# Gradient of w_mod in an adaLN block: its sixth row moved behind the last fold, four rows of the last stage on VectorE

## The chip, the cores and the metric

The kernel runs on one core of a Trainium2 chip. A core has five engines with instruction queues of their own: TensorE (PE, matrix products, with the weight load PEld), VectorE (DVE), ScalarE (ACT), GpSimd (POOL) and SyncE (SP, which here only issues DMA transfers; POOL and ACT issue some too). An engine works through its queue in order; an instruction that waits holds up all behind it. Queues wait for each other through semaphores. The metric is the device time of one execution in microseconds, the median of several runs.

## The reference, cut to what matters

The kernel computes the forward pass and all gradients of one block with x of 2048 x 1024 tokens in bf16:

```python
mod = (_silu(c) @ w_mod).reshape(c.shape[0], 6, 1, -1)
sa, ca, ga, sb, cb, gb = (mod[:, k].copy() for k in range(6))
h = _layernorm(x) * (1 + ca) + sa
x = x + ga * irfft2(rfft2(h) * (w_r + 1j * w_i))
h = _layernorm(x) * (1 + cb) + sb
x = x + gb * (gelu(_layernorm(h) @ w1 + b1) @ w2 + b2)
...
_out, _vjp = jax.vjp(_f, A_x, A_w_r, A_w_i, B_w1, B_b1, B_w2, B_b2, c, w_mod)
```

(`...` marks what is left out.) The change concerns the last two gradients. With u = silu(c) and g_r the gradient of the r-th of the six vectors sa, ca, ga, sb, cb, gb (1024 numbers each), the gradient of `w_mod` is, for each row r of the six, the outer product of u and g_r (1024 x 1024), and the gradient of c needs, for each row r, the product of w_mod's r-th block with g_r.

## The kernel before

The forward part is followed by the backward part, in which PE has one matrix product after another. Three stages matter here.

*Fold stage* (about 940 to 1000 us): the last of four quarters of the token gradients is brought back through the two layer norms (`ln_bwd`, by DVE reduces and ACT instructions with result in `got`), folded by DVE for the Fourier products (`fold_quarter`, whose last instruction is `fold_end`), and turned (`turn_tokens`). `make_fm` then scales the small matrices `fm` on DVE. Meanwhile PE computes products of the gradient of `w2` (`gw2acc`), one unit at a time, wherever the code says `fill(n)`: `pieces()` is a generator of such units, and every `fill` takes some. Each product of 16 matmuls goes into one of four PSUM tiles of tag `f` and is evicted from there by ACT (or, early on, DVE) into `gwo` or `gwoE`.

*Spectral core* (to about 1180): Fourier products, with `U` (CE, SE from ACT's copies of `pu`; CO, SO from DVE sums of `smbf`), the pairs with `ws` and `cs01b`, and the gradient of the filter.

*Last stage* (1185 to the end): `consume_bwd(i, ...)` finishes the four token quarters i = 0 to 3. In each, DVE unfolds, multiplies by the normalised x (`tmp = o4 * n1`, the column-sum product), goes back through the first layer norm (`scaled_rows`, `ln_bwd`) and adds `d_gx1`, which SP loads into the place of `n1` (tile `xt`, line 1483). PE fills with the 56 products of the gradient of `w1` (`gw1acc`, line 1553), each 16 matmuls into a PSUM tile of tag `f`; ACT evicts each into one of eight slots `gwo` (line 1557), and POOL stores it (line 1559). The operands `gzh` and `gzu` come by transposing transfers on SP (line 1502).

Row 3 of the gradient of `w_mod` is done in the spectral core (`row3`). The five others stand in the last stage, in `gmod_steps`: for each row r SP loads g_r, spread over the partitions, into `gr` (line 1172), and then there are eight steps of 128 lines of `w_mod`. A step loads 128 x 1024 numbers of `w_mod` into one of four slots `wrw` (line 1176); makes the outer product, u as a scale per partition times `gr`, into a slot of `otl` (rows 2, 4, 5 on ACT, line 1179, behind the last eviction, three slots; rows 1, 0 on DVE, line 1181, two slots); stores it through POOL (line 1182); and reduces `wrw` times `gr` on DVE into one column of `gu` (line 1183). Two chains, rows 5, 4, 2 and rows 1, 0, are taken in turn, a step of each per `fill(1)` from the ninth on.

Between the two stands row 0's own gradient: PE sums columns into `accSA`, ACT scales that into `sr` (line 1607). `sr` lies in the place (`px0`) that `xt` of quarter 3 had.

The order on each engine follows from the order in the code and a scheduler; `tc.issue_after(x)` keeps an instruction behind x on its own engine's order, `tc.high_priority()` moves evictions ahead. Tiles of the pool `reg` have a tag each, one place per tag: a new tile of a tag waits until the earlier one is done with.

Of the kernel before, what the change touches and what calls it, by code (L numbers as in the profile page):

```python
# [35 lines left out]
def kernel(  # L36
# [157 lines left out]
    def tt(out, a, b, op):  # L194
        return nc.vector.tensor_tensor(out=out, in0=a, in1=b, op=op)  # L195
# [975 lines left out]
    def gmod_steps(r, wrs, gws, gr):  # L1171
        nc.sync.dma_start(out=gr, in_=d_gmod[r * D:(r + 1) * D].partition_broadcast(P))
        for jc in range(NDC):
            wr, gw = wrs[:, wring[0] % 4, :], gws[jc % len(gws)]
            wring[0] += 1
            nc.sync.dma_start(out=wr, in_=w_mod[jc * P:(jc + 1) * P, r * D:(r + 1) * D])
            if r > 1:
                with tc.issue_after(w1g["ev"].ins):
                    nc.scalar.activation(out=gw, in_=gr, func=ACT.Identity, scale=u_rt[:, jc:jc + 1])  # L1179
            else:  # L1180
                nc.vector.tensor_scalar(out=gw, in0=gr, scalar1=u_rt[:, jc:jc + 1], scalar2=None, op0=ALU.mult)
            nc.gpsimd.dma_start(out=out_9[jc * P:(jc + 1) * P, r * D:(r + 1) * D], in_=gw)  # L1182
            nc.vector.tensor_tensor_reduce(out=wr, in0=wr, in1=gr, scale=1.0, scalar=0.0,  # L1183
                                           op0=ALU.mult, op1=ALU.add, accum_out=gu[:, r, jc:jc + 1])
            yield
# [59 lines left out]

    def ln_bwd(g, gsum, n_ap, tmp, order=ExitStack):
        sc = small.tile([P, 1], FP32, tag="lbsc", bufs=4)
        nc.vector.tensor_tensor_reduce(out=tmp, in0=g, in1=n_ap, scale=-1.0 / D, scalar=0.0,  # L1248
                                       op0=ALU.mult, op1=ALU.add, accum_out=sc[:])
        with order():  # L1250
            nc.scalar.activation(out=tmp, in_=n_ap, func=ACT.Identity, scale=sc[:], bias=gsum)  # L1251
        tt(g, g, tmp, ALU.add)
# [163 lines left out]
    def make_fm():  # L1416
        for r in range(2):
            cos, ncos = al[:, 1, r:r + 1], al[:, 4, r:r + 1]
            for k in range(2):
# [3 lines left out]
                for t in range(2):  # L1423
                    nc.vector.tensor_scalar(out=fv[:, t, :, 1, :], in0=em2[:, 2 + r + 4 * t, 255:P - 1:-1].rearrange("p (h j) -> p h j", h=2),
                                            scalar1=cos if t == k else ncos, scalar2=None, op0=ALU.mult)

# [33 lines left out]
    css2 = reg.tile([P, 2, 2, 2 * PW], BF16, name="cs01b", tag="px0")  # L1460
    with tc.issue_after(gx_in[0].ins):
        nc.gpsimd.memset(css2[:], 0.0)
    accCA = []

    def consume_bwd(i, o4, tmp, tmp2, n1, eb):
# [10 lines left out]
        tt(tmp, o4, n1, ALU.mult)  # L1476
# [6 lines left out]
        nc.sync.dma_start(out=n1, in_=chunk_rows(d_gx1, i))  # L1483
        tt(o4, o4, n1, ALU.add)
        store_tok(out_1, o4, i)
        fill((4, 1, 2, 2)[i])
# [19 lines left out]
    def pieces():  # L1506
# [34 lines left out]
        w1g["gr"] = reg.tile([P, 2, D], BF16, name="gr", tag="sb")  # L1541
        w1g["gr2"] = reg.tile([P, 2, D], BF16, name="gr2", tag="gm")
# [29 lines left out]
    for cl in (CE, SE):  # L1572
        nc.sync.dma_start(out=smA2[:, cl // 2], in_=d_SF[:, cl])
    sums3(3, gn3s[1], pru)
    nc.sync.dma_start(out=em2, in_=d_E[:, 0])
    fill(8)
    with tc.issue_after(fold_end[0].ins):
        make_fm()
# [27 lines left out]
    for h in range(2):  # L1606
# [54 lines left out]
```

## Time and profile before

| what | value |
|---|---|
| median of 3 runs | 1410.78 us |
| lowest and highest run | 1408.07 and 1412.80 us |
| profiled execution | 1409.95 us |
| its span, first to last instruction | 1407.9 us |
| mean granted clock of TensorE | 0.992 |
| data moved by DMA | 331.12 MB, 235 GB/s over the span |

In a row of the timeline there stand: start in the span, duration, engine, line, operation, output and inputs, and how many instructions were merged; in square brackets how long the engine stood idle before, and what ended it. In a row of the windows: the window, its length, busy time of PE, PEld, DVE, ACT and POOL with their numbers of instructions, TensorE's granted clock as a share of full speed, the DMA engines' busy share, and GB/s. In a row of the waits: who waited for whom, microseconds in total, how often, the longest. In a row of the groups: line, engine, operation, shapes and count; busy time and mean ns of one; idle time before, and what ended it.

### The profile page before, as it was taken

The page shows a single profiled execution, that of the slowest core. Times are in us where ns is not written, and L with a number is a line of the kernel's source. Part 1 is how long each engine was busy: PE and PEld are TensorE (multiplying, and loading weights), DVE is VectorE, ACT ScalarE, POOL GpSimd, SP SyncE. Part 2 cuts the span into 40 slices and gives each one's busy share as a digit, 9 for nine tenths or more (in the row PEclk, how much of TensorE's full clock was granted, in tenths as well). Part 3 has the DMA queues.
Part 4 walks back from the last instruction along what each step waited for, and adds up shares of the span by engine and source line. Part 5 has one row for each costly group of instructions (what it writes and reads, how often), then busy time and mean ns, then how long its engine had stood idle before and what let it go on. Part 6 is the DMA issues. An engine that isn't in the chain of part 4 may idle for free. (4 is left out here: it accounts for less than half of the span.)

```text
span 1407.9 us, 18600 instructions
## 1 busy us (share of the span) xinstructions
PE 1360.4 (97%) x6899; PEld 655.9 (47%) x6899; DVE 1058.4 (75%) x1455; ACT 783.1 (56%) x1106; POOL 344.1 (24%) x434
## 2 busy tenths in 40 slices
PE   4898999999999999999999999999999999999888
PEld 2445565444444444444444444444645564544333
DVE  5897889977888787887620578889687679877871
ACT  4775657667867766665314593443623555443335
POOL 5410523201212122112211011111254130322333
PEclk9999999999999999999999999999999999999999
DMA  9972746799787777697999599995399697879884
GB/s 315 287 235 65 199 135 197 253 302 357 243 254 227 236 239 242 191 275 249 279 283 242 153 245 321 264 258 146 119 287 262 164 284 184 228 197 232 280 304 175
DMA packets 360688, 331.12 MB, mean 235 GB/s; under 512 B 207962, under 2 KB 303088, under 8 KB 360470
## 3 DMA queue, kind: packets, MB, share of 16 engines
q1 hardware_dynamic: 319702, 204.96, 55.7%
q0 software_dynamic: 35136, 119.73, 24.5%
q10 hardware_dynamic: 5760, 5.25, 1.2%
q8 instruction: 54, 0.88, 0.3%
q14 instruction: 36, 0.29, 0.1%
HBM read 165.73 MB, written 114.87 MB: 199 GB/s over the span
## 5 line engine op out<-in xcount | busy, mean ns | idle before, releaser
L839 PE MATMUL pp<-gBoT,wt 128*128 128x512 bf16 x896 | 198.6, 380 | 2.5 <-ACT phr L845 1.2
L1130 PE MATMUL pg<-w1T,gzr 128*128 128x512 bf16 x896 | 195.8, 379 | 0.0
L1553 PEld LDWEIGHTS <-n3n 128*128 128x128 bf16 x896 | 88.6, 99 | 120.2 <-issue 19.5
L1553 PE MATMUL gw1acc<-gzh,n3n 128*128 128x512 bf16 x640 | 140.0, 379 | 1.2 <-ACT gwo L1557 1.2
L976 PEld LDWEIGHTS <-w 128*128 128x128 bf16 x896 | 87.3, 98 | 107.7 <-issue 3.3
L839 PEld LDWEIGHTS <-wt 128*128 128x128 bf16 x896 | 87.6, 98 | 106.7 <-issue 5.2
L1130 PEld LDWEIGHTS <-gzr 128*128 128x128 bf16 x896 | 86.6, 98 | 108.4 <-issue 5.5
L976 PE MATMUL pz<-n3Tb,w 128*128 128x512 bf16 x448 | 99.2, 379 | 1.9 <-DVE w2sD L1052 1.9
L976 PE MATMUL pz<-n3Ta,w 128*128 128x512 bf16 x448 | 98.7, 379 | 0.0
L195 DVE TENSOR_TENSOR ct<-ct 128x2048 bf16<-128x2048 bf16 (+1 forms) x84 | 91.4, 1117 | 5.6 <-DMA d_n<-ct 3.1
L1030 PEld LDWEIGHTS <-hhA 128*128 128x128 bf16 x608 | 59.0, 98 | 73.1 <-issue 2.9
L1294 PE MATMUL gw2acc<-gB,hhsA 128*128 128x512 bf16 x416 | 92.4, 379 | 0.0
L979 ACT ACTIVATE gt<-pz,b_col 128x512 bf16<-128x512 f32 x112 | 72.8, 683 | 33.3 <-PE pz L976 33.0
L987 ACT ACTIVATE gt<-gt 128x2048 bf16<-128x2048 bf16 x28 | 53.5, 1911 | 64.6 <-DVE gt L195 64.6
L195 DVE TENSOR_TENSOR gt<-gt,gt 128x2048 bf16<-128x2048 bf16 x56 | 68.6, 1224 | 19.8 <-ACT gt L989 18.5
L1302 ACT CAST gwo<-gw2acc 128x512 bf16<-128x512 f32 x40 | 23.5, 588 | 87.5 <-PE gw2acc L1294 70.3
L1553 PE MATMUL gw1acc<-gzu,n3n 128*128 128x512 bf16 x256 | 60.9, 402 | 9.3 <-ACT gwo L1557 9.2
L1294 PEld LDWEIGHTS <-hhsA 128*128 128x128 bf16 x416 | 40.8, 98 | 47.1
L1183 DVE CUSTOM_DVE_ANT_0 wrw<-wrw,gr 128x1024 bf16<-128x1024 bf16 x40 | 48.0, 1219 | 18.8 <-DMA wrw<-in_w_mod_dram 18.4
L1557 ACT CAST gwo<-gw1acc 128x512 bf16<-128x512 f32 x56 | 32.0, 575 | 50.3 <-PE gw1acc L1553 42.3
L983 ACT ACTIVATE gt<-gt 128x2048 bf16<-128x2048 bf16 x28 | 53.5, 1910 | 3.2 <-DVE hhC L195 2.4
L989 ACT ACTIVATE gt<-gt 128x2048 bf16<-128x2048 bf16 x28 | 53.4, 1907 | 0.4
(367 smaller groups left out, 2515.0 us busy)
## 6 DMA issues: line engine op xcount, KB each, us to landing
gzr<-d_gz SPq DMA_DIRECT2D x28, 512.0 KB
wblk<-in_w_mod_dram SPq DMA_DIRECT2D x12, 1024.0 KB
out_dram<-otl POOLq DMA_DIRECT2D x48, 256.0 KB
d_ph<-pho POOLq DMA_DIRECT2D x21, 512.0 KB
wrw<-in_w_mod_dram SPq DMA_DIRECT2D x40, 256.0 KB
d_hh<-hhA POOLq DMA_DIRECT2D x19, 512.0 KB
w<-in_B_w_dram SPq DMA_DIRECT2D x7, 1024.0 KB
hhC<-d_ph SPq DMA_DIRECT2D x14, 512.0 KB
```

The costliest lines, as they stand in the source:

```text
L195: return nc.vector.tensor_tensor(out=out, in0=a, in1=b, op=op)
L839: last_pe[0] = nc.tensor.matmul(pp[:], lhsT=wt[:, fc % 4, cch, :], rhs=gBoT[j][:, cch, :], start=(cch == 0), stop=(cch == NDC - 1))
L976: last_pe[0] = nc.tensor.matmul(pz[:], lhsT=w1s[g][:, cch, k * P:(k + 1) * P], rhs=n3T[:, cch, :], start=(cch == 0), stop=(cch == NDC - 1))
L979: z_in = nc.scalar.activation(out=zb[:, k, :], in_=pz[:], func=ACT.Identity, bias=b1_col[:, fc:fc + 1], scale=1.0)
L983: nc.scalar.activation(out=av, in_=zb, func=ACT.Square)
L987: nc.scalar.activation(out=sg, in_=bv, func=ACT.Sigmoid, scale=2.0 * GK)
L989: nc.scalar.activation(out=bv, in_=bv, func=ACT.Sigmoid, scale=-2.0 * GK)
L1030: last_pe[0] = nc.tensor.matmul(pbs[i][:], lhsT=hh[:, k, i * P:(i + 1) * P], rhs=wp[:, k, :], start=False, stop=(g == 6 and k == 3))
L1130: last_pg[0] = nc.tensor.matmul(pgs[i][:], lhsT=gzs[b, g][:, k, i * P:(i + 1) * P], rhs=w1Ts[g][:, k, h * KH:(h + 1) * KH], start=(g == 0 ...
L1183: nc.vector.tensor_tensor_reduce(out=wr, in0=wr, in1=gr, scale=1.0, scalar=0.0, op0=ALU.mult, op1=ALU.add, accum_out=gu[:, r, jc:jc + 1])
L1294: nc.tensor.matmul(acc[:], lhsT=hh_of(fc)[:, t, :], rhs=gBs[t // 4][:, t % 4, h * KH:(h + 1) * KH], start=(t == 0), stop=(t == NT - 1))
L1553: nc.tensor.matmul(acc[:], lhsT=n3ns[t // 4][:, t % 4, cch * P:(cch + 1) * P], rhs=gz2[t // 8][:, t % 8, :], start=(t == 0), stop=(t == NT ...
```

## The change

Row 5 leaves the last stage. Its `gr5` and the first four loads of `w_mod` (`wr5a`) are issued on SP behind the loads of `smf`, the other four (`wr5b`) behind a load of the `w2` product. Its eight outer products are made on ACT behind the last `ln_bwd` instruction of the fold stage, into four slots `gw5`, and stored by POOL; its eight reduces stand on DVE behind `make_fm`. The memset of `css2` on POOL goes behind the last of those stores.

Rows 4, 2, 1, 0 become one chain, `gmod_chain`: all outer products and reduces on DVE, five slots of `otl` for all, four of `wrw`, and the load for step n + 4 issued with step n. Its first four loads stand on SP behind the `xt` load of quarter 1. The steps stand behind the column-sum product of quarter 3 on DVE: two per `fill(1)` for the first eight, one for the other sixteen.

```diff
-    def gmod_steps(r, wrs, gws, gr):
...
+    def gmod_chain(rows):
+        steps = [(r, k, jc) for k, r in enumerate(rows) for jc in range(NDC)]
+
+        def load(n):
+            r, k, jc = steps[n]
+            if jc == 0:
+                nc.sync.dma_start(out=w1g["gr"][k], in_=d_gmod[r * D:(r + 1) * D].partition_broadcast(P))
+            nc.sync.dma_start(out=w1g["wr"][:, n % 4, :], in_=w_mod[jc * P:(jc + 1) * P, r * D:(r + 1) * D])
+
+        for n in range(4):
+            load(n)
+        yield
+        for n, (r, k, jc) in enumerate(steps):
+            wr, gw, gr = w1g["wr"][:, n % 4, :], w1g["gw"][n % 5], w1g["gr"][k]
             nc.vector.tensor_tensor_reduce(out=wr, in0=wr, in1=gr, scale=1.0, scalar=0.0,
                                            op0=ALU.mult, op1=ALU.add, accum_out=gu[:, r, jc:jc + 1])
+            nc.vector.tensor_scalar(out=gw, in0=gr, scalar1=u_rt[:, jc:jc + 1], scalar2=None, op0=ALU.mult)
+            nc.gpsimd.dma_start(out=out_9[jc * P:(jc + 1) * P, r * D:(r + 1) * D], in_=gw)
+            if n + 4 < len(steps):
+                load(n + 4)
             yield
...
-    with tc.issue_after(gx_in[0].ins):
-        nc.gpsimd.memset(css2[:], 0.0)
...
+    chain = gmod_chain((4, 2, 1, 0))
...
-        tt(tmp, o4, n1, ALU.mult)
+        prod_in[0] = tt(tmp, o4, n1, ALU.mult)
...
-        nc.sync.dma_start(out=n1, in_=chunk_rows(d_gx1, i))
+        x1_in = nc.sync.dma_start(out=n1, in_=chunk_rows(d_gx1, i))
...
+        if i == 1:
+            with tc.issue_after(x1_in.ins):
+                next(chain)
...
-    fill(8)
+    gr5 = reg.tile([P, D], BF16, name="gr5", tag="sb")
+    wr5 = [reg.tile([P, 4, D], BF16, name="wr5a", tag="t1"), None]
+    gw5 = reg.tile([P, 4, D], BF16, name="gw5", tag="uv0")
...
+    for jc in range(NDC):
+        fill(1)
+        with tc.issue_after(ln_act[0].ins):
+            nc.scalar.activation(out=gw5[:, jc % 4, :], in_=gr5[:], func=ACT.Identity, scale=u_rt[:, jc:jc + 1])
+        st5 = nc.gpsimd.dma_start(out=out_9[jc * P:(jc + 1) * P, 5 * D:6 * D], in_=gw5[:, jc % 4, :])
...
     with tc.issue_after(fold_end[0].ins):
-        make_fm()
+        fm_in = make_fm()
+    with tc.issue_after(fm_in.ins):
+        for jc in range(NDC):
+            wr = wr5[jc // 4][:, jc % 4, :]
+            nc.vector.tensor_tensor_reduce(out=wr, in0=wr, in1=gr5[:], scale=1.0, scalar=0.0,
+                                           op0=ALU.mult, op1=ALU.add, accum_out=gu[:, 5, jc:jc + 1])
...
-    chains = [(r for row, k in ((5, 0), (4, 1), (2, 0)) for r in gmod_steps(row, w1g["wr"], w1g["gw"][0:3], w1g["gr"][:, k, :])),
-              (r for row, k in ((1, 0), (0, 1)) for r in gmod_steps(row, w1g["wr"], w1g["gw"][3:5], w1g["gr2"][:, k, :]))]
     for n in range(24):
         fill(1)
-        with tc.issue_after(w1g["ins"].ins):
-            for chain in chains[0:1 if n < 8 else 2]:
+        with tc.issue_after(w1g["ins"].ins), tc.issue_after(prod_in[0].ins):
+            for _ in range(2 if n < 8 else 1):
                 next(chain)
```

PE's instructions stand in the same order before and now. Three places where the others moved follow; lines 1251, 1305, 1483, 1502 and 1557 of before are 1259, 1313, 1492, 1514 and 1569 now.

ACT at the end of the last stage; `gwo` are the slots of the evictions, `otl` those of the outer products, `sr` the scaled column sums of row 0. Before (the last two rows go on in turn):

```order
L233 COPY ct<-accCA 64x512
L1557 CAST gwo_9596<-gw1acc 128x512 x2
L1607 ACTIVATE sr<-accSA_10429 1x512
L1607 ACTIVATE sr<-accSA_10430 1x512
L1557 CAST gwo_9596<-gw1acc 128x512
L1179 ACTIVATE otl<-gr,u_rt 128x1024
```

Now, to the end of the queue:

```order
L233 COPY ct<-accCA 64x512
L1569 CAST gwo_9633<-gw1acc 128x512 x2
L1645 ACTIVATE sr<-accSA_10471 1x512
L1645 ACTIVATE sr<-accSA_10472 1x512
L1569 CAST gwo_9633<-gw1acc 128x512 x26
```

The 24 outer products of rows 5, 4 and 2 are gone from between the evictions.

SP around the `xt` load of quarter 3 (`d_gx` is the token gradient, `gzh` the operands of the last group of `w1` products). Before:

```order
L1502 DMA_TRANSPOSE gzh_9592<-d_gz 128x8x512
L1502 DMA_TRANSPOSE gzh_9593<-d_gz 128x8x512
L1172 DMA gr<-d_gmod 128x1024
L1176 DMA wrw<-in_w_mod_dram 128x1024 x4
L1172 DMA gr<-d_gmod 128x1024
L1176 DMA wrw<-in_w_mod_dram 128x1024 x2
L1483 DMA xt<-d_gx_99 128x4x1024
```

Now:

```order
L1514 DMA_TRANSPOSE gzh_9630<-d_gz 128x8x512
L1178 DMA wrw<-in_w_mod_dram 128x1024
L1177 DMA gr<-d_gmod 128x1024
L1178 DMA wrw<-in_w_mod_dram 128x1024
L1492 DMA xt<-d_gx_99 128x4x1024
```

Six w_mod loads and two `gr` stood between the transposes and `xt`, now two and one; the first `gr` and four loads of row 4 stand behind the `xt` load of quarter 1.

ACT in the fold stage (`gwoE` are evictions of `w2` products, `n3u` the turned tokens). Before:

```order
L1305 CAST gwoE<-gw2acc 128x512
L1251 ACTIVATE got<-n2u,s2c,sc 128x1024 x2
L1305 CAST gwoE<-gw2acc 128x512 x4
L1164 ACTIVATE n3u<-fbuf_6236,al 128x1024
L1163 ACTIVATE n3u<-fbuf_6236,al 128x1024 x2
```

Now, with `gw` the slots `gw5`:

```order
L1313 CAST gwoE<-gw2acc 128x512
L1259 ACTIVATE got<-n2u,s2c,sc 128x1024 x2
L1602 ACTIVATE gw_7563<-gr_7561,u_rt 128x1024 x4
L1313 CAST gwoE<-gw2acc 128x512
L1602 ACTIVATE gw_7563<-gr_7561,u_rt 128x1024 x2
L1313 CAST gwoE<-gw2acc 128x512
L1602 ACTIVATE gw_7563<-gr_7561,u_rt 128x1024 x2
L1313 CAST gwoE<-gw2acc 128x512 x2
```

Row 5's eight outer products stand between four evictions: four ahead of the first, two ahead of each of the next two.

More of the change, by code (lines that the diff above doesn't have):

```diff
@@ L1244, in ln_sums @@
         nc.vector.tensor_scalar(out=gs, in0=gs, scalar1=-1.0 / D, scalar2=None, op0=ALU.mult)
+    ln_act = [None]
     def ln_bwd(g, gsum, n_ap, tmp, order=ExitStack):
@@ L1250, in ln_bwd @@
         with order():
-            nc.scalar.activation(out=tmp, in_=n_ap, func=ACT.Identity, scale=sc[:], bias=gsum)
-        tt(g, g, tmp, ALU.add)
+            ln_act[0] = nc.scalar.activation(out=tmp, in_=n_ap, func=ACT.Identity, scale=sc[:], bias=gsum)
+        return tt(g, g, tmp, ALU.add)
     def scaled_rows(out4, in4, row, gs, r, b):
@@ L1540, in pieces @@
         w1g["gw"] = [otl[:, k * D:(k + 1) * D] for k in (0, 1, 2, 3, 5)]
-        w1g["gr"] = reg.tile([P, 2, D], BF16, name="gr", tag="sb")
-        w1g["gr2"] = reg.tile([P, 2, D], BF16, name="gr2", tag="gm")
+        grs = [reg.tile([P, 2, D], BF16, name="gr", tag=tag) for tag in ("sb", "gm")]
+        w1g["gr"] = [g[:, k, :] for g in grs for k in range(2)]
         gw1_load(0)
```

30 lines of the change are left out of this document (16 added, 14 removed).

## The prediction

> **What bounds the kernel now.** I read first whom TensorE (PE) waits for from 900 us on, since the page has PE busy for 97% of the span:
>
> ```profile
> PE 1360.4 (97%) x6899; PEld 655.9 (47%) x6899; DVE 1058.4 (75%) x1455; ACT 783.1 (56%) x1106; POOL 344.1 (24%) x434
> PE gw1acc L1553 <- ACT gwo L1557: 10.4, 3, 5.0
> PE pcs L581 <- ACT smbf L806: 0.2, 1, 0.2
> ```
>
> These two are all of PE's waits there: three for ScalarE's (ACT's) eviction of a finished product. PE's timeline places them:
>
> ```profile
> 1262.36 27.79 PE L1553 MATMUL gw1acc<-gzh,n3n 128*128 128x512 bf16 x128
> 1290.08 0.61 PE L218 MATMUL accCA<-ct,ones_bf 128*32 128x512 bf16 x8
> 1297.98 7.07 PE L1553 MATMUL gw1acc<-gzh,n3n 128*128 128x512 bf16 x32
> 1304.88 7.07 PE L1553 MATMUL gw1acc<-gzu,n3n 128*128 128x512 bf16 x32
> 1316.91 34.27 PE L1553 MATMUL gw1acc<-gzu,n3n 128*128 128x512 bf16 x144 [4.96 <-ACT gwo L1557]
> 1355.43 19.69 PE L1553 MATMUL gw1acc<-gzu,n3n 128*128 128x512 bf16 x80 [4.25 <-ACT gwo L1557]
> 1374.96 3.62 PE L1553 MATMUL gw1acc<-gzh,n3n 128*128 128x512 bf16 x16
> 1379.74 24.33 PE L1553 MATMUL gw1acc<-gzh,n3n 128*128 128x512 bf16 x112 [1.16 <-ACT gwo L1557]
> 1404.00 0.22 PE L210 MATMUL ptr<-fin,gc_bf 128*8 128x128 bf16 x1
> ```
>
> Undisturbed, 128 matmuls take 1290.08 - 1262.36 = 27.72 us, 0.2166 each. From 1297.98 to 1404.00 there are 32 + 32 + 144 + 80 + 16 + 112 = 416; at that pace 90.1 us, in fact 106.0. **The loss is 15.9 us**: 10.4 of waiting and 5.5 in which PE ran slowly. The windows show where:
>
> ```profile
> 1305.00:1315.00 10.00, 6.95 (x33) 3.02 (x31) 8.20 (x12) 0.00 (x0) 0.00 (x0) 1.00 0.82 262
> 1315.00:1325.00 10.00, 8.09 (x25) 3.14 (x25) 10.00 (x20) 6.08 (x9) 6.19 (x6) 0.66 0.84 284
> 1355.00:1365.00 10.00, 9.57 (x34) 3.83 (x34) 7.46 (x16) 4.45 (x6) 3.75 (x7) 0.75 0.90 305
> ```
>
> The column behind the engines is the granted clock: 0.66 and 0.75 right behind the two long stalls. Of the loss, 1351.18 - 1297.98 - 208 x 0.2166 = 8.1 us belong to the first stall, 7.8 to the other two. What held ACT:
>
> ```profile
> 1297.79 0.58 ACT L1557 CAST gwo<-gw1acc 128x512 bf16<-128x512 f32 x1 [0.96 <-ACT gwo L1557]
> 1315.34 1.06 ACT L1607 ACTIVATE sr<-accSA 1x512 f32<-1x512 f32 x2 [16.96 <-DVE ct L195]
> 1316.31 0.56 ACT L1557 CAST gwo<-gw1acc 128x512 bf16<-128x512 f32 x1
> 1353.76 1.15 ACT L1179 ACTIVATE otl<-gr,u_rt 128x1024 bf16<-128x1024 bf16 x1 [6.25 <-issue]
> 1378.07 1.15 ACT L1179 ACTIVATE otl<-gr,u_rt 128x1024 bf16<-128x1024 bf16 x1 [3.77 <-DMA out_dram<-otl]
> 1305.48 0.38 SPq L1483 DMA_DIRECT2D xt<-d_gx  x1
> 1312.87 2.29 DVE L195 TENSOR_TENSOR ct<-ct,xt 128x4096 bf16<-128x4096 bf16 x1 [1.80 <-DMA xt<-d_gx]
> ```
>
> First stall: the two L1607 instructions stand ahead of the next eviction and reuse `xt`'s place, so they wait until VectorE (DVE) has added `xt`; its load left SyncE's queue (SP) only at 1305.48, behind w_mod loads that wait for DVE's reduces. The other two: outer products L1179 that wait for the landing of a store stand ahead of evictions.
>
> **Last stage, removed.** PE's order is unchanged, and no L1179 is left on ACT: behind the `sr` pair stand 26 evictions alone. Stalls two and three lose their cause: -7.8 us.
>
> **First stall.** It goes if the `xt` addition starts early enough. From its start to PE's restart are 1316.91 - 1312.87 = 4.04 us; PE needs its buffer at 1316.91 - 4.96 = 1311.95, so it must start by 1307.9.
>
> ```profile
> 1279.60 16.02 SPq L1502 DMA_TRANSPOSE gzh<-d_gz  x2
> 1295.68 0.57 SPq L1172 DMA_DIRECT2D gr<-d_gmod  x1
> 1296.30 2.74 SPq L1176 DMA_DIRECT2D wrw<-in_w_mod_dram  x4
> 1302.37 2.68 SPq L1176 DMA_DIRECT2D wrw<-in_w_mod_dram  x2
> 1301.11 1.22 DVE L1183 CUSTOM_DVE_ANT_0 wrw<-wrw,gr 128x1024 bf16<-128x1024 bf16 x1 [7.77 <-DMA wrw<-in_w_mod_dram]
> 1293.26 0.08 DVE L1248 DVE_READ_ACCUMULATOR2_ANT sc<- 128x1 f32 x1
> L195 DVE TENSOR_TENSOR ct<-ct 128x1024 bf16<-128x1024 bf16 x4 | 2.7, 686 | 0.0
> ```
>
> Before, `xt` stood behind six w_mod loads, and the fifth and sixth of them each waited for a reduce, the first of which came only at 1301.11, when its own load had landed. Now row 4's first `gr` and four loads leave around 1221, behind the `xt` load of the second quarter, so that only one w_mod load, one `gr` and one more w_mod load stand between the transposes (done 1295.6) and `xt`. The second of these loads waits for the second reduce. DVE's last L1248 ends at 1293.3; the first reduce, now ahead of the row scaling, shifts that to 1294.5; one outer product (0.5) and the second reduce (1.2) end at 1296.2. With 0.6 to 0.7 us of SP's time for each load `xt` leaves near 1297.5, and with the 7.4 us of before (1305.48 to 1312.87) its addition can start at 1304.9. DVE itself must come that far: three more reduces, four outer products, the four `ct` additions and the row sum that stood there before are 3.7 + 1.9 + 2.7 + 0.7 = 9.0 us from 1296.2, so 1305.2. The last of those reduces needs the load issued at 1295.7; the load of 1296.30 was used at 1301.11, so it is there. Start 1305.2 against 1307.9: 2.7 us to spare. Lower bound of the cost: no stall; upper bound: the whole 8.1 us, as before. I take no stall, because the two rows that set the start, the departure of `xt` and the first reduce, both move by 8 us or more. What is late next on ACT is the `sr` pair itself, done near 1308.6, with three evictions piled up behind it at 0.56 us each; the four PSUM tiles carry that.
>
> What moves at 1221 costs SP about 3 us ahead of transposes for products that start at 1304.88; the SP row of 1279.60 shows that the queue still issues transposes 25 us ahead of that. I put nothing for it.
>
> **Added to DVE there.** Groups of the stage:
>
> ```profile
> L1183 DVE CUSTOM_DVE_ANT_0 wrw<-wrw,gr 128x1024 bf16<-128x1024 bf16 x40 | 48.0, 1219 | 18.8 <-DMA wrw<-in_w_mod_dram 18.4
> L1179 ACT ACTIVATE otl<-gr,u_rt 128x1024 bf16<-128x1024 bf16 x24 | 27.6, 1150 | 39.6 <-DMA out_dram<-otl 32.7 <-issue 6.2 <-ACT gwo L1557 0.7
> L1181 DVE TENSOR_SCALAR otl<-gr,u_rt 128x1024 bf16<-128x1024 bf16 x16 | 7.7, 480 | 1.4 <-DMA out_dram<-otl 1.4
> ```
>
> 32 reduces and 32 outer products on DVE are 32 x (1.22 + 0.48) = 54.4 us, against 48.0 + 7.7 = 55.7 before: row 5's eight reduces leave as much as the 16 added products bring. So DVE is no fuller, and ACT is rid of 27.6 us. What sets the pace of a step is the traffic: before, 40 reduces ran from 1301.1 to 1377.3, 1.9 each, with 18.4 us of waits for loads. At the `xt` addition five of the 32 steps are done; the other 27 at 1.9 us from 1307.5 end at 1359, inside PE's run, which lasts to 1297.98 + 90.1 = 1388. What hides them is the cover between a step and PE: four PSUM tiles and eight output slots. Without that cover PE would stop for the output stores, which stand in POOL's queue between those of the steps; that is the slower rival below.
>
> **Row 5 in the fold stage.** Eight ACT products, eight DVE reduces, 17 transfers of 256 KB.
>
> ```profile
> 965.48 0.56 ACT L1305 CAST gwoE<-gw2acc 128x512 bf16<-128x512 f32 x1
> 968.64 0.58 ACT L1305 CAST gwoE<-gw2acc 128x512 bf16<-128x512 f32 x1 [2.60 <-PE gw2acc L1294]
> 972.10 0.58 ACT L1305 CAST gwoE<-gw2acc 128x512 bf16<-128x512 f32 x1 [2.87 <-PE gw2acc L1294]
> 990.16 0.52 DVE L1424 TENSOR_SCALAR smbf<-empf,al 128x128 bf16<-128x128 bf16 x2
> 998.48 0.68 DVE L195 TENSOR_TENSOR rows<-acc3b,au 64x512 bf16<-64x512 f32 x1 [7.80 <-ACT au L233]
> 1002.21 5.16 DVE L195 TENSOR_TENSOR U<-smbf 128x512 bf16<-128x512 bf16 x8 [3.05 <-ACT smbf L806]
> 986.79 0.54 POOL L561 DMA_DIRECT2D ws<-in_A_w_r_dram  x1 [9.82 <-DVE smbf L1424]
> 940.00:1000.00 60.00, 60.00 (x327) 29.77 (x326) 48.21 (x71) 28.72 (x41) 14.43 (x17) 1.00 0.57 151
> ```
>
> ACT first. Four products of 1.15 us stand ahead of the eviction of 965.48 and make it 4.6 us late; two more stand ahead of each of the next two. Evictions come 3.46 us apart, so with four PSUM tiles one may be 3 x 3.46 = 10.4 us late before PE stops. The later products reuse the four slots and wait for their stores: with 4 to 5 us for a store (the load above took 4.8), the fifth starts near 971, the seventh, whose store stands behind the 1 MB of `d_gx` on POOL, near 979, and the third eviction is some 9 us late, the fourth 6. Bounds: 0, or 3 us if the stores take half as long again. I take 0.2, nearer the hidden end, since the cover holds in all three places.
>
> DVE next: 990.68 + 8 x 1.22 + 0.68 = 1001.1, ahead of `U` at 1002.21. The two gaps of 7.80 and 3.05 us hide it, with 1.1 us left; if the loads are late and this cover goes, each microsecond more reaches PE, for the 0.2 us wait for `smbf` in the first fence shows no slack behind it. The second half of the loads waits on SP for the store of `d_gx` (about 978) and then has 17 us before DVE wants it at 995.
>
> POOL gets eight store issues, and the memset that stood ahead moves behind them, into the gap of 9.82 us that ends with `ws`. The 17 transfers, 4.25 MB, meet DMA engines 57% busy at 151 GB/s, half of what the windows above reach (284). On SP they stand behind loads that are needed sooner.
>
> **Sum.** Profiled execution 1409.95 us (span 1407.9): 1409.95 - 7.8 - 8.1 + 0.2 = 1394.2. It lies 0.8 below the median of the runs, 1410.78, so I forecast **1395**.
>
> **The rivals.** *A stall remains* (0.17). `xt`, or a late eviction in the fold stage, still stops PE for a while. For it: only 2.7 and about 1.4 us of slack stand at the end of chains of a dozen waits. Against: the starts of both chains are known from rows that do not move. The first stall whole costs 8.1 us and gives 1403; 2 us of it cost 2 x 15.9/10.4 = 3.1, 1398. The Trainium skill, "TensorE: Matmul & The Clock Gate", section "What's actually happening", says that the array's clock drops only after an idle window of about 3.4 us; the trace agrees, since behind the stall of 1.16 us 112 matmuls took 24.33, full pace. By that rule a remainder of 2 us would cost 2 us and the time be 1397.
>
> *Nothing gained* (0.08): the loss returns elsewhere, the same ring at about 3.0 us a step or the fold stage stopping PE for as long as the last stage does now; about 1410. For it: PE is full from 940 to 1298, so that any delay there counts whole. Against: the 15.9 us sit at ACT instructions that are gone or released earlier, and in the fold stage the gaps are there in the rows.
>
> *Slower* (0.13): the steps become a ring that paces PE. In it SP's load waits for the reduce four steps back, DVE's outer product for the store five steps back, POOL, in order, for each outer product, ACT's eviction for the output store eight products back, and PE for the eviction. The store of the twelfth product after 1298 stands behind the last step's; the eviction that reuses its slot falls due at 1367, and PE stops 10.4 us after that. With 5 us for the store the last step must end by 1372.5: (1372.5 - 1307.5)/27 = 2.4 us a step. From 3.2 us on PE loses 21.6 us and the time is 1394.2 + 21.6 = 1416. For it: L1179 spent 32.7 us waiting for stores, and here DVE would do that waiting with its reduces queued behind. Against: 1.9 us a step before, with the same traffic, and five slots in place of three and two.
>
> **How the numbers follow.** Forecast 0.62 (its own range 1391.5 to 1397.5), the rivals 0.17, 0.08, 0.13. A measurement tells 0.3% (4.2 us) from no change: faster means below 1406.6, slower above 1415.0. Faster: 0.62 + 0.17 = 0.79; same 0.08; slower 0.13. The range 1391.5 to 1406 holds the first two.
>
> **What would show it.** Right: no PE wait for an eviction behind 1298, clock 1.00 in all windows to the end, `xt` issued near 1298, PE's last product near 1388, the last reduce before 1370. Wrong: a PE wait around 965 to 1015 for ACT; `sr` after 1310; steps over 2.7 us apart with evictions waiting for output slots.

## The result and the profile after

The changed kernel takes 1399.17 us, the median of six runs (1394.43 to 1400.33), beside 1410.93 for the kernel before; the ratio is 0.9917 with a 95% interval of 0.9895 to 0.9939. That is faster by 11.8 us, and 4.2 us above the forecast of 1395: within the stated range of 1391.5 to 1406, but outside the forecast's own 1391.5 to 1397.5. The profiled execution took 1398.61 us, 4.4 above the sum of 1394.2 that was made for it; its span is 1396.8, its mean granted clock 0.990.

Whom PE waits for from 900 us on, in the changed kernel (the page's busy line first; waits of less than 0.4 us left out):

```profile
PE 1351.6 (97%) x6774; PEld 657.6 (47%) x6899; DVE 1063.7 (76%) x1471; ACT 767.6 (55%) x1090; POOL 347.8 (25%) x434
...
PE gw1acc L1565 <- DVE ct L779: 2.8, 1, 2.8
PE pu L1445 <- ACT smbf L806: 0.6, 2, 0.4
```

The three waits for ACT's evictions are gone. In their place stands one for a DVE instruction that the prediction does not name. PE's timeline shows where:

```profile
1258.82 0.61 PE L218 MATMUL accCA<-ct,ones_bf 128*32 128x512 bf16 x8
...
1277.93 17.43 PE L1565 MATMUL gw1acc<-gzh,n3n 128*128 128x512 bf16 x79 [2.83 <-DVE ct L779]
1302.75 0.59 PE L215 MATMUL accSA<-otl,ones_bf 128*128 128x512 bf16 x2
...
1310.09 55.42 PE L1565 MATMUL gw1acc<-gzu,n3n 128*128 128x512 bf16 x251
1365.34 27.79 PE L1565 MATMUL gw1acc<-gzh,n3n 128*128 128x512 bf16 x126
1393.06 0.22 PE L210 MATMUL ptr<-fin,gc_bf 128*8 128x128 bf16 x1
```

(Some matmul records are missing from this trace: 251 stand for 256, 126 for 128; the times are not touched by that.) Two marks cut the stage for all that follows: `accCA` of quarter 2, here at 1258.82, and `accSA`, here at 1302.75. The kernel before has the same two at 1256.60 and here:

```profile
1297.55 0.59 PE L215 MATMUL accSA<-otl,ones_bf 128*128 128x512 bf16 x2
```

From `accSA` to PE's last product the kernel before needs 1404.00 - 1297.55 = 106.45 us, the changed one 1393.06 - 1302.75 = 90.31. **So 16.1 us are gained there, where 15.9 were forecast.** Between the marks 2.98 us are lost: 1302.75 - 1258.82 = 43.93 us in place of 40.95 (1297.55 - 1256.60). Of these, 2.83 are the new wait. Another 2.2 us lie ahead of 1258 (1258.82 against 1256.60); they come back below.

The chain that the first stall hung on, in the changed kernel: the load of `xt` leaves SP, DVE adds it, ACT makes `sr`; the last row is DVE's last reduce.

```profile
1302.54 1.93 SPq L1492 DMA_DIRECT2D xt<-d_gx  x1
1311.62 2.29 DVE L195 TENSOR_TENSOR ct<-ct,xt 128x4096 bf16<-128x4096 bf16 x1 [1.46 <-DMA xt<-d_gx]
1314.09 1.06 ACT L1645 ACTIVATE sr<-accSA 1x512 f32<-1x512 f32 x2 [9.58 <-DVE ct L195]
1359.00 1.22 DVE L1185 CUSTOM_DVE_ANT_0 wrw<-wrw,gr 128x1024 bf16<-128x1024 bf16 x1
```

By the prediction the addition had to start by 1307.9, which is 10.35 us behind `accSA`; here it starts 8.9 behind it, 1.5 us in time, where 2.7 to spare were forecast. Two windows that were slow before and the groups of the stage (from 1285 us) after:

```profile
1315.00:1325.00 10.00, 9.95 (x48) 4.53 (x47) 10.00 (x22) 3.33 (x7) 6.35 (x10) 1.00 0.94 336
1355.00:1365.00 10.00, 9.95 (x47) 4.55 (x47) 6.17 (x15) 1.75 (x3) 6.63 (x13) 1.00 0.76 284
```

```profile
L1185 DVE CUSTOM_DVE_ANT_0 wrw<-wrw,gr 128x1024 bf16<-128x1024 bf16 x32 | 38.9, 1214 | 1.4 <-DMA wrw<-in_w_mod_dram 1.3
L1187 DVE TENSOR_SCALAR otl<-gr,u_rt 128x1024 bf16<-128x1024 bf16 x32 | 15.8, 494 | 0.0
```

The clock is 1.00 throughout. DVE waits 1.3 us for loads (18.4 before) and not at all for stores.

The fold stage, first ACT's products of row 5 and evictions, then DVE's last reduce of row 5 and the first `U`, then PE:

```profile
966.89 4.25 ACT L1602 ACTIVATE gw<-gr,u_rt 128x1024 bf16<-128x1024 bf16 x4
971.05 0.56 ACT L1313 CAST gwoE<-gw2acc 128x512 bf16<-128x512 f32 x1
...
981.33 1.05 ACT L1313 CAST gwoE<-gw2acc 128x512 bf16<-128x512 f32 x2
999.91 1.23 DVE L1612 CUSTOM_DVE_ANT_0 wr5b<-wr5b,gr 128x1024 bf16<-128x1024 bf16 x1
1003.51 5.16 DVE L195 TENSOR_TENSOR U<-smbf 128x512 bf16<-128x512 bf16 x8 [1.77 <-ACT smbf L806]
1001.71 3.66 PE L1445 MATMUL pu<-smbf,fbuf 128*128 128x256 bf16 x32
```

PE's product `pu` stands 1.29 us later than before (1001.71 against 1000.42), as late as PE was at 940 already (1.35). So the eight products and eight reduces cost PE nothing here.

**The new wait.** Quarter 2, in the kernel before: two transposes of `gzu` and a store of `ct` on SP; then ACT's last layer-norm instruction, which frees the place of `xt`, and SP's load into it.

```profile
1220.98 12.27 SPq L1502 DMA_TRANSPOSE gzu<-d_gz  x2
1233.35 0.53 SPq L165 DMA_DIRECT2D out_dram<-ct  x1
...
1261.34 1.24 ACT L1251 ACTIVATE ct<-xt,s1c,sc 128x1024 bf16<-128x1024 bf16 x1
1262.60 0.36 SPq L1483 DMA_DIRECT2D xt<-d_gx  x1
```

The same in the changed kernel, with SP's store and transposes ahead of the load, DVE's addition and the DVE eviction of `po` that stands behind it:

```profile
1261.39 1.24 ACT L1259 ACTIVATE ct<-xt,s1c,sc 128x1024 bf16<-128x1024 bf16 x1
1235.65 0.53 SPq L165 DMA_DIRECT2D out_dram<-ct  x1
1236.27 18.45 SPq L1514 DMA_TRANSPOSE gzu<-d_gz  x1
1254.82 13.49 SPq L1514 DMA_TRANSPOSE gzh<-d_gz  x2
1268.41 0.52 SPq L1492 DMA_DIRECT2D xt<-d_gx  x1
1274.98 2.29 DVE L195 TENSOR_TENSOR ct<-ct,xt 128x4096 bf16<-128x4096 bf16 x1 [11.62 <-DMA xt<-d_gx]
1277.19 0.68 DVE L779 CAST ct<-po 128x512 bf16<-128x512 f32 x1
```

ACT freed the place at 1262.6 in both. Before, the load left at once; now SP was in its transposes until 1268.4, 5.8 us longer, and PE waited for the PSUM tile that the `po` eviction frees. Two things differ on SP ahead of that: the early loads stand in front of the `gzu` transposes, and the store of `ct`, which stood behind both, now stands between them. Without the 2.83 us the addition would have had to start by 1272.15, 13.3 us behind `accCA` of quarter 2: a second limit of the same kind as the 10.35 us behind `accSA`.

### The profile page after: what moved, and what is told of

The parts are those of the page before. It is cut to its first block, busy times and chain, and to the rows that moved or that the text cites. A ratio compares the mean times of both kernels' runs of the same rounds, so it can differ in the third digit from the quotient of the medians.

```text
span 1396.8 us, 18464 instructions
## 1 busy us (share of the span) xinstructions
PE 1351.6 (97%) x6774; PEld 657.6 (47%) x6899; DVE 1063.7 (76%) x1471; ACT 767.6 (55%) x1090; POOL 347.8 (25%) x434
## 4 chain that ended last, share of the span: by engine, by line
PE 72%; DVE 7%; DMA 3%; issue 1%; ACT 1%; ACTq 0%; DVEq 0%
PE pg L1130 14%; PE gw1acc L1565 13%; PE gw2acc L1302 13%; PE pz L976 13%; PE pbo L1030 13%; DVE ct L195 4%; PE pp L839 2%; PE po L774 1%; DVE st L493 1%; PE pcs L581 1%; DMA hhsA<-d_hh 1%; DMA w2sA<-in_B_w_dram 1%; DMA d_n<-ct 1%; PE acc3a L218 1%; PE pu L542 1%
## 5 line engine op out<-in xcount | busy, mean ns | idle before, releaser
L195 DVE TENSOR_TENSOR gt<-gt,gt 128x2048 bf16<-128x2048 bf16 x56 | 68.6, 1224 | 19.8 <-ACT gt L989 18.5
L1565 PE MATMUL gw1acc<-gzu,n3n 128*128 128x512 bf16 x251 | 55.2, 379 | 0.3
L1302 PE MATMUL gw2acc<-gB,otl 128*128 128x512 bf16 x218 | 49.2, 379 | 0.4 <-issue 0.2
```

The lines of the kernel that those rows point to most:

```text
L1302: nc.tensor.matmul(acc[:], lhsT=hh_of(fc)[:, t, :], rhs=gBs[t // 4][:, t % 4, h * KH:(h + 1) * KH], start=(t == 0), stop=(t == NT - 1))
L1565: nc.tensor.matmul(acc[:], lhsT=n3ns[t // 4][:, t % 4, cch * P:(cch + 1) * P], rhs=gz2[t // 8][:, t % 8, :], start=(t == 0), stop=(t == NT ...
```

## The experiments

Eleven runs, on the chip beside runs of the kernel before. Each leaves the computation whole.

| run | median, runs | ratio to before, 95% | `accSA` to PE's end |
|---|---|---|---|
| the change, first measured | 1399.17, 6 | 0.9917, 0.9895 to 0.9939 | 90.31 |
| e1 `xt` first | 1405.78, 10 | 0.9973, 0.9955 to 0.9992 | 100.92 |
| e2 products on DVE | 1395.64, 4 | 0.9897, 0.9865 to 0.9929 | 90.31 |
| e3 row 5 back | 1397.49, 6 | 0.9912, 0.9888 to 0.9937 | 94.97 |
| e4 early loads later | 1397.66, 6 | 0.9916, 0.9887 to 0.9945 | 90.31 |
| e5 the change again | 1398.53, 6 | 0.9922, 0.9894 to 0.9950 | 90.31 |
| e6 as e4 again | 1394.75, 6 | 0.9893, 0.9874 to 0.9912 | 90.32 |
| e7 products on DVE, `xt` first | 1395.42, 6 | 0.9898, 0.9880 to 0.9917 | 90.32 |
| e8 as e3, loads later | 1397.13, 6 | 0.9901, 0.9880 to 0.9922 | 90.31 |
| e9 two output slots | 1401.08, 3 | 0.9939, 0.9909 to 0.9968 | 91.15 |
| e10 row 5 alone | 1405.65, 10 | 0.9974, 0.9956 to 0.9993 | 99.61 |
| e11 no early loads | 1400.05, 6 | 0.9924, 0.9903 to 0.9945 | 96.94 |

The last column is from one profiled execution each (the kernel before: 106.45). Runs of one kernel spread by 3 to 12 us, so the marks tell kernels apart better than the medians.

**e1: the `xt` load first, alone.**

```diff
+        x1_in[0] = nc.sync.dma_start(out=n1, in_=chunk_rows(d_gx1, i))
...
-        with tc.issue_after(w1g["ins"].ins):
+        with tc.issue_after(w1g["ins"].ins), tc.issue_after(x1_in[0].ins):
             for chain in chains[0:1 if n < 8 else 2]:
```

> The kernel before with one edit: the w_mod loads of the last stage stand on SP behind the xt load of quarter 3, no longer ahead of it; the outer products stay where they were, 24 of them on ACT. Theory (two separate losses, 8.1 and 7.8 us): xt leaves SP near 1297 and no longer at 1305.5, the first PE wait (5.0 us) and its slow clock go, the waits behind ACT's outer products stay at 4 to 6 us in total; 1410.9 - 8.1 = 1403. Rival (one loss: the evictions are late by the outer products whatever xt does, the stall only moves back): PE waits in the last stage still sum to 9 us or more, 1409 to 1411.

PE's timeline in e1, its rows with a wait in the last stage:

```profile
1343.62 3.62 PE L1554 MATMUL gw1acc<-gzu,n3n 128*128 128x512 bf16 x16 [1.84 <-ACT gwo L1558]
1349.03 3.61 PE L1554 MATMUL gw1acc<-gzu,n3n 128*128 128x512 bf16 x16 [1.80 <-ACT gwo L1558]
1356.73 16.38 PE L1554 MATMUL gw1acc<-gzu,n3n 128*128 128x512 bf16 x64 [4.09 <-ACT gwo L1558]
```

`xt` left at 1297.81 and the first stall is gone, but the later waits grew from 5.4 to 7.7 us and the loss from `accSA` on fell by 5.5 us (106.45 to 100.92), not by 8.1. Neither theory holds whole: the losses are two, but the second grows when the first is taken out.

**e2: all outer products on DVE, alone.**

```diff
-            if r > 1:
-                with tc.issue_after(w1g["ev"].ins):
-                    nc.scalar.activation(out=gw, in_=gr, func=ACT.Identity, scale=u_rt[:, jc:jc + 1])
-            else:
-                nc.vector.tensor_scalar(out=gw, in0=gr, scalar1=u_rt[:, jc:jc + 1], scalar2=None, op0=ALU.mult)
+            nc.vector.tensor_scalar(out=gw, in0=gr, scalar1=u_rt[:, jc:jc + 1], scalar2=None, op0=ALU.mult)
```

> The kernel before with one edit: all 40 outer products of the last stage on DVE, none on ACT; row 5 stays in the last stage, no load is early. Theory: the second and third PE wait go (-7.8 us); of the first, a part stays, since in this order xt stands on SP behind one load that waits for a reduce, where it were two: it leaves near 1302.7 and not 1305.5, so the wait is 5.0 - 2.8 = 2.2 us; time 1398 to 1401. Rival (the ring of steps sets the pace once DVE does everything): 40 steps at 2.4 us or more, evictions that wait for output slots, 1409 or slower.

In e2: SP's load, `accSA`, the addition, the last reduce of 40.

```profile
1304.24 0.62 SPq L1479 DMA_DIRECT2D xt<-d_gx  x1
1302.29 0.59 PE L215 MATMUL accSA<-otl,ones_bf 128*128 128x512 bf16 x2
1311.83 2.29 DVE L195 TENSOR_TENSOR ct<-ct,xt 128x4096 bf16<-128x4096 bf16 x1 [0.29 <-DMA xt<-d_gx]
1376.52 1.23 DVE L1179 CUSTOM_DVE_ANT_0 wrw<-wrw,gr 128x1024 bf16<-128x1024 bf16 x1 [0.34 <-DMA wrw<-in_w_mod_dram]
```

No wait from `accSA` on: the whole gain, 16.1 us, without row 5's move and without early loads, where a rest of 2.2 us was expected. `xt` left 1.5 us later than expected, but PE came to `accSA` 4.7 us later than in the profile of before, while the transposes on SP ended only 0.8 us later (1296.4), so the addition, 9.5 us behind `accSA`, was within the 10.35. It was PE's lateness in this profile that spared it the rest; a PE 0.9 us earlier would have waited. The ring rival is refuted: 40 steps on DVE end at 1377.7, 15 us ahead of PE.

**e3: row 5 back in the last stage.**

```diff
-    chain = gmod_chain((4, 2, 1, 0))
+    chain = gmod_chain((5, 4, 2, 1, 0))
...
-            for _ in range(2 if n < 8 else 1):
+            for _ in range(2 if n < 16 else 1):
```

> The changed kernel with row 5 back in the last stage, as the first row of the one chain on DVE (40 steps); the fold stage is as in the kernel before; the early loads stand where the change has them (they are row 5's now). Theory: DVE has room for 40 steps at the 1.5 to 1.7 us of the changed kernel (end near 1375 of 1393), so moving row 5 brought nothing: within 1 us of the changed kernel, 1399, with the same PE wait of 2.8 us near 1278. Rival (the last stage was too full, and row 5's eight steps are what the change had to take out): steps run late, PE waits for evictions behind 1330, 3 us or more slower than the changed kernel.

The rows of PE with a wait from 1258 us on, the addition of `xt` in quarter 3, and the window behind it:

```profile
1277.86 17.43 PE L1569 MATMUL gw1acc<-gzh,n3n 128*128 128x512 bf16 x80 [1.05 <-DVE ct L779]
...
1319.91 50.19 PE L1569 MATMUL gw1acc<-gzu,n3n 128*128 128x512 bf16 x224 [2.81 <-ACT gwo L1573]
1315.87 2.29 DVE L195 TENSOR_TENSOR ct<-ct,xt 128x4096 bf16<-128x4096 bf16 x1 [5.77 <-DMA xt<-d_gx]
1320.00:1325.00 5.00, 5.00 (x16) 1.89 (x16) 5.00 (x10) 1.29 (x3) 3.86 (x7) 0.66 0.88 292
```

The profiled execution, 1403.21, is the slowest of the six; the others lie at 1396.1 to 1397.9, so the median is the change's own or a little less, as the theory has it. Near 1278 PE waited 1.05 us and not the 2.8 expected. The wait of 2.81 us in quarter 3, which was not expected, is no lack of room for steps: the transposes of `gzh` ended late (1302.4), `xt` left at 1305.40, and the addition started 13.2 us behind `accSA` (1302.69), 2.8 over the limit. No wait stands behind 1320, so the rival fails.

**e4 and e6: the early loads behind the `gzu` transposes. e5: the change again.**

```diff
-        if i == 1:
-            with tc.issue_after(x1_in.ins):
-                next(chain)
...
                 w1g["ins"] = gw1_load(k)
+                if k == 5:
+                    with tc.issue_after(w1g["k0"].ins):
+                        next(chain)
```

(`k0` is the first of the two transposes of that call, here the second `gzu` that SP issues.)

> The changed kernel with one edit: row 4's early gr and four w_mod loads stand on SP behind the gzu transpose of about 1236 and no longer ahead of the one of 1227; SP and the DMA engines have a gap there in the kernel before. Theory (these loads push the transposes and so the xt load of quarter 2 from 1262.6 to 1268.4, DVE's addition of it and the eviction of po that stands behind): xt leaves by 1265.5 at PE's present shift of 2.2 us, the PE wait of 2.8 us near 1278 goes, 2.5 to 3 us faster than the changed kernel, 1396. Rival (xt is late for row 5's transfers or for the order of the store and the transposes): the wait stays above 2 us, 1399. Second rival: the loads push gzh instead, the same wait.

> The changed kernel once more, unchanged, beside the three that follow on one chip. Theory (the early loads cause the PE wait near 1278): the wait is there again, 1 to 3 us, with the xt load of quarter 2 leaving SP 4 us or more after ACT's last layer-norm instruction of that quarter; from the accCA product of quarter 2 (1258.8) to the end of PE 134.5 us. Rival (that wait was one execution's chance): no wait there, 131.5 us.

> The changed kernel with the early gr and four w_mod loads behind the gzu transposes, once more. Theory: no PE wait from 1258 to the end; 131.5 us from the accCA product of quarter 2 to PE's end, and a median 2 to 3 us under that of the changed kernel on this chip. Rival (the loads' place is worth nothing in most executions): medians within 1 us.

SP in e4, and PE's longest row:

```profile
1236.86 2.72 SPq L1178 DMA_DIRECT2D wrw<-in_w_mod_dram  x4
...
1265.26 0.38 SPq L1492 DMA_DIRECT2D xt<-d_gx  x1
...
1306.73 55.42 PE L1566 MATMUL gw1acc<-gzu,n3n 128*128 128x512 bf16 x256
```

The same loads, 1.25 MB, put into a gap of SP, delay nothing: `xt` of quarter 2 leaves 0.03 us after ACT has freed its place (1265.23), in e6 too, and PE has no wait from 940 on except 0.2 us. From `accCA` of quarter 2 to the end PE takes 131.25 us in e4 and 131.43 in e6, against 134.24 in the change's first profile. In e5 the same `xt` load was late again (1266.54, ACT done at 1263.82), but its addition started 12.8 us behind `accCA`, 0.6 within the limit, and PE did not wait: 131.26 us. So the theory holds for the delay, and the rival for the wait: with the early loads in front of the `gzu` transposes `xt` is late by 2.7 to 5.8 us each time, and whether PE feels it is decided by a microsecond. Four profiles have the loads in that place; the waits in them are 2.83 (the change), 1.05 (e3), 0 (e5) and 0.62 (e9), 1.1 on average. The nine profiles without them there have none of this kind, and `xt` is not late. One rival is not separated from this: in the same four programs the store of `ct` stands between the two `gzu` transposes, and the transpose right behind it holds SP for 10.5 to 18.5 us; in the nine others it stands behind both. No run moves the loads without the store, so whether the loads' own 3.3 us on SP or the store's new place makes the delay is open. The medians, 1394.75 (e6) against 1398.53 (e5) beside the same runs of before, lean the same way with intervals that overlap.

**e7 and e8: is row 5's move needed?** e7 is e1 and e2 together, e8 is e3 with the loads of e4.

> The kernel before with two edits: all 40 outer products of the last stage on DVE, and the xt load of quarter 3 ahead of the w_mod loads on SP. Row 5 stays, nothing is loaded early. Theory (the two edits together carry the whole gain, and the steps have room): xt leaves SP within 1 us of ACT's last layer-norm instruction, no PE wait from 1298 to the end, the last reduce near 1378 of 1392; as far below before as e2, 12 to 13 us (1396 at 1408.4 for before). Rival (the later start of the steps makes the ring the limit): the last reduce after 1385, PE waits for evictions, 3 us or more above e2.

> The changed kernel with row 5 back as the first row of the one chain on DVE and the early loads behind the gzu transposes. Theory: neither the wait near 1278 nor one near 1319 (2.8 us in e3, where xt left late); from the accCA product of quarter 2 to the end of PE 131.5 us as in e4; time as e6 within 1 us, so that the move of row 5 is worth nothing. Rival (row 5 in the fold stage is worth something once the early loads are out of the way): 2 us or more above e6.

In both PE never waits from 1017 us to the end; from `accCA` of quarter 2 they take 131.26 and 131.25 us. The last reduce starts at 1378.89 in e7 and 1369.89 in e8, ahead of PE's end at 1389.33 and 1391.57. Both theories hold on the marks: 40 steps fit, and moving row 5 is worth nothing there. e8's median lies 2.4 us above e6's, which is the sign that its rival named (the intervals overlap). In the profiles PE was 2.3 us later at 940 already (943.14 against 940.87), ahead of anything that differs, and from there to its end PE takes 448.43 us in both, the fold stage included; so the profiles give the move no worth, and the difference of the medians stays unexplained. e7, two small edits of the kernel before, beats the kernel before and lies about 3 us below the change run beside it, as e6 does; the intervals overlap, so 3 us is a tendency.

**e9: two output slots in place of five.**

```diff
-            wr, gw, gr = w1g["wr"][:, n % 4, :], w1g["gw"][n % 5], w1g["gr"][k]
+            wr, gw, gr = w1g["wr"][:, n % 4, :], w1g["gw"][n % 2], w1g["gr"][k]
```

> The changed kernel with two output slots for the outer products in place of five. Theory (the ring of the slower rival is real, and five slots keep the steps out of it): a product waits for the store two steps back, some 5 to 6.5 us, so that steps come 2.5 to 3.3 us apart and no longer 1.5; from 1313 on the 27 steps end at 1381 to 1402, past the 1378 from which evictions wait for output slots; PE waits in the last stage, 5 to 25 us slower than the changed kernel. Rival (the steps are paced by DVE alone and the stores land within 3 us): steps stay under 2 us apart, no PE wait, same time as the changed kernel.

DVE's outer products in e9 from 1313 us on, the product ahead of the `xt` addition, that addition, the last reduce, and PE's only wait behind `accSA`:

```profile
L1187 DVE TENSOR_SCALAR otl<-gr,u_rt 128x1024 bf16<-128x1024 bf16 x29 | 14.0, 484 | 17.0 <-DMA out_dram<-otl 16.8
1312.89 0.49 DVE L1187 TENSOR_SCALAR otl<-gr,u_rt 128x1024 bf16<-128x1024 bf16 x1 [3.70 <-DMA out_dram<-otl]
1315.44 2.27 DVE L195 TENSOR_TENSOR ct<-ct,xt 128x4096 bf16<-128x4096 bf16 x1
1366.31 1.22 DVE L1185 CUSTOM_DVE_ANT_0 wrw<-wrw,gr 128x1024 bf16<-128x1024 bf16 x1
1319.46 48.51 PE L1565 MATMUL gw1acc<-gzu,n3n 128*128 128x512 bf16 x219 [0.68 <-ACT gwo L1569]
```

DVE now waits 16.8 us for stores, but the steps still end at 1367.5, 1.8 us apart from the addition's end (1317.7) on, since a store took 3.3 us (the median from issue to landing) and not 5 to 6.5. One eviction stood 0.8 us for an output slot (its row starts at 1361.97), which PE did not feel. PE's 0.68 us are the `xt` limit again: the addition started at 1315.44, 11.1 us behind `accSA` at 1304.38. It did not wait for its load; DVE had stood 3.70 us at a store just ahead of it. So two slots do reach PE, by this way and for 0.68 us. The rival holds in the steps' pace, but not in its reason (DVE alone) and not quite in "no PE wait". The ring of the slower rival, in which evictions stop PE, is still far off with two slots. The median above the change's is not explained by it: in this profile ACT's late copies `smbf` near 1155 cost 4.1 us.

**e10: row 5 moved, nothing else. e11: the change without early loads.**

```diff
-    chains = [(r for row, k in ((5, 0), (4, 1), (2, 0)) for r in gmod_steps(row, w1g["wr"], w1g["gw"][0:3], w1g["gr"][:, k, :])),
+    chains = [(r for row, k in ((4, 0), (2, 1)) for r in gmod_steps(row, w1g["wr"], w1g["gw"][0:3], w1g["gr"][:, k, :])),
```

(e10: with row 5's part as the change has it.) e11:

```diff
-        if i == 1:
-            with tc.issue_after(x1_in.ins):
-                next(chain)
...
+    with tc.issue_after(w1g["ins"].ins):
+        next(chain)
     for n in range(24):
```

> The kernel before with row 5 moved as in the change, and nothing else: rows 4 and 2 stay on ACT in the last stage, no early load, xt behind six w_mod loads. Theory (row 5 was not what bound the last stage): the first PE wait is there as before, 4 to 5 us, and at least one of the later two (16 products on ACT still wait for stores); from the accSA product to PE's end 100 us or more of 106.5; time 1405 to 1410 where before is 1409 to 1410. Rival (fewer steps, so the later waits go): 98.7 us from accSA to the end, 1402.

> The changed kernel without the early loads: row 4's gr and first four w_mod loads stand on SP behind the last gzh transposes, ahead of one more gr, one more load and the xt load of quarter 3. Theory (two rules read from the traces: PE waits near 1278 if the xt addition of quarter 2 starts later than 13.3 us behind the accCA product of that quarter, and near 1318 if that of quarter 3 starts later than 10.4 us behind the accSA product): the first of the two waits does not come; xt of quarter 3 leaves SP 4 to 7 us behind accSA and its addition starts 11 to 14 us behind it, so the second comes with 1 to 4 us; 1397 to 1400. Rival (xt is early enough without them, since only one load in front of it waits for a reduce): no PE wait at all, 1395.

e10's theory missed on the first wait: it was not there, since SP's transposes ended early (1290.7) and the addition started 9.8 us behind `accSA`. Three waits behind outer products remain (1.0, 1.4 and 4.6 us), and 9.3 us of the loss (99.61 from `accSA` to the end, where 100 or more was expected). e11, its wait and its addition of quarter 3:

```profile
1319.42 1.44 PE L1562 MATMUL gw1acc<-gzu,n3n 128*128 128x512 bf16 x3 [5.04 <-ACT gwo L1566]
1315.38 2.29 DVE L195 TENSOR_TENSOR ct<-ct,xt 128x4096 bf16<-128x4096 bf16 x1 [0.57 <-DMA xt<-d_gx]
```

As the theory has it, quarter 2 has no wait, and in quarter 3 the addition came 15.4 us behind `accSA` (1299.97), 5.1 over the limit; PE waited 5.04, a little above the 1 to 4 expected, since `xt` left 7.9 us behind `accSA` and not 4 to 7. With these loads back between the transposes and `xt`, the old first stall is back at full length.

The limit of 10.35 us (worked out from the first row) against all profiles in which PE waited for this addition, and the nearest in which it did not:

| profile | addition behind `accSA` | over 10.35 | PE waited |
|---|---|---|---|
| before | 15.32 | 4.97 | 4.96 |
| e11 | 15.41 | 5.06 | 5.04 |
| e3 | 13.18 | 2.83 | 2.81 |
| e9 | 11.06 | 0.71 | 0.68 |
| e10 | 9.78 | none | none |
| e2 | 9.54 | none | none |
| the change | 8.87 | none | none |

Apart from the loads in front of `xt` (and, in e9, DVE's wait for a store), what moves it is the end of SP's transposes, which is not tied to PE: it lies from 6.0 us ahead of `accSA` (e10) to level with it (e11). The kernel before and e10 have the same order there; the transposes end 1.9 and 6.0 us ahead, and the addition starts 15.3 and 9.8 us behind.

## Why the prediction was right, and where not

*The time.* 1399.17 lies where the rival "a stall remains" was priced (2 us of it at 1398), and the profile shows that a stall did remain. But it is not the one that the rival named: it stands at the `xt` load of quarter 2, and not of quarter 3 or in the fold stage. Its length is chance: with the early loads in the same place PE waited between 0 and 2.83 us. Nor is it the whole of the 4.2 us, since e5's profile, which has no such wait, took 1397.59, 3.4 above the sum.

*The loss and its going.* Measured 16.1 us where 15.9 was forecast, with the mechanism that was named: no outer product between evictions, `xt` issued at `accSA`, its addition in time, clock 1.00. The margin was thin: 1.5 us in this profile, 2.6 in e5 (7.8 us behind `accSA`). The limit for the addition, worked out from one stall, held in every other profile to a few hundredths of a microsecond.

*The split into 8.1 and 7.8* was wrong as a sum of independent terms. `xt` first alone brought 5.5 us (e1), products on DVE alone all 16.1 in its profile (e2). When PE is no longer held up earlier, the waits behind products that wait for stores grow (5.4 to 7.7 us in e1); and the first stall is there or not by where SP's transposes happen to end.

*The early loads* are the step that failed: "What moves at 1221 costs SP about 3 us ahead of transposes for products that start at 1304.88 ... I put nothing for it." I looked at who needs those transposes, not at what stands behind them on SP, the `xt` load of quarter 2, nor at what stands behind its addition on DVE, an eviction of `po` that PE needs. It cost 3.0 us in the profiled execution (2.83 of waiting) and between 0 and 2.83 in four profiles. Nor was it 3 us of SP: the load came 5.8 us late, and the loads brought a store of `ct` in front of a transpose with them, whose share no run shows. Put into the gap 12 us later, the same loads cost nothing (e4, e6, e8); left out, they brought the first stall back (e11). Something of the kind was needed: these loads at another place, or `xt` first as in e7.

*Row 5 in the fold stage*, put at 0.2: measured nothing, on the way that was described. The eviction of 965.48, now at 971.05, is 4.2 us late beyond PE's own 1.35 (forecast 4.6), the third 7.9 (forecast 9). DVE was ready for `U` 1.8 us ahead (forecast 1.1). But the move was not needed (e2, e7, e8).

*The pace of a step* was mis-sized: 1.9 us, set by the traffic, against (1360.2 - 1313.9)/27 = 1.7, nearly DVE's own 1.21 + 0.49. That the last reduce ended at 1360.2, near the forecast 1359, is two misses that cancel: the 27 steps began 6.4 us later than forecast (1313.9 against 1307.5) and took 5 us less. With that pace the ring of the slower rival was further off than its 0.13 allowed for; even two slots (e9) cost PE only 0.68 us.

*What is left of the 4.4 us* between the sum and the profiled execution: 3.0 from the early loads; 1.35 that PE was late at 940 already, ahead of everything changed; 0.9 near 1150, where ACT's copies `smbf` came late. Against these stand 0.2 each from the fold stage and the last stage, and 0.4 less outside PE's run. The 0.9 stays open: ACT stood idle there until it had issued a store of `gwo` (3.30 us in the changed kernel, 7.04 in e9). It held PE up in six of the 13 profiles, among them e2, whose program up to that place is that of before; in none of e4, e6 and e8, nor in the only profile of before. Whether that is chance the runs do not tell.

## What to carry to other kernels

A transfer moved to an earlier place on a queue is priced by everything behind it there, followed to the first instruction that the bottleneck engine waits for, and not by who uses the transfers that it passes; look also at what else changes its order with it. In a gap of the queue the same loads cost nothing here. A stall gives a limit, the latest start of the instruction that ends it, counted from a mark on the bottleneck engine; that number carries over to other versions, while stalls counted one by one do not add up. Before work is moved to another stage, try whether changing its engine alone is enough.

## What the runs showed of the hardware

The granted clock fell behind a wait of 2.81 us (e3, 0.66 in the window 1320 to 1325 above) and did not behind one of 2.83 us in the changed kernel:

```profile
1280.00:1285.00 5.00, 5.00 (x25) 2.25 (x23) 4.93 (x5) 0.59 (x1) 2.31 (x5) 1.00 1.15 240
```

So nearly the same wait cost 4.66 us in e3 (94.97 - 90.31) and 2.98 in the changed kernel. The clock fell also behind a wait of only 1.87 us (e3, for `smbf`, ending at 1151.73), and not behind one of 3.31 us at the same product in e9:

```profile
1150.00:1155.00 5.00, 3.18 (x20) 2.29 (x20) 2.80 (x5) 3.71 (x8) 0.33 (x1) 0.81 1.05 377
```

In the 13 profiles, from 100 us on, no wait of 0.9 to 1.84 us was followed by a slower clock, every wait of 3.60 us or more was, and between these it went either way. The Trainium skill, "TensorE: Matmul & The Clock Gate", section "What's actually happening", puts the idle time after which the clock drops at about 3.4 us; here it dropped eight times behind shorter waits.

Busy DMA engines may move little. In the changed kernel, between 1250 and 1255, while SP was held in its transposes, they were busier than in the kernel before at 1235, at less than a third of the rate (of 5,209 packets between 1236 and 1256, 4,428 had under 512 B). First the changed kernel, then the one before:

```profile
1250.00:1255.00 5.00, 4.95 (x24) 2.23 (x23) 4.96 (x8) 0.59 (x1) 0.03 (x1) 1.00 1.16 125
```

```profile
1235.00:1240.00 5.00, 5.00 (x25) 2.26 (x24) 0.00 (x0) 1.10 (x2) 2.54 (x4) 1.00 1.03 402
```
